# A chunked linear-attention layer and a product feed-forward on one core: a new written-out order, w loaded by SyncE, y in separate steps

## The chip, the cores and the metric

The kernel runs on one core of a Trainium2 chip. The metric is the device time of one execution in microseconds (us). The engines are TensorE (PE, with its weight loads PEld), VectorE (DVE), ScalarE (ACT), GpSimd (POOL) and SyncE (SP). SP and POOL issue the transfers.

## The reference

Inputs r, k, v, w have shape (batch 4, heads 8, steps 768, 48), in float32. For each batch and head a state of 48 x 48 runs over the steps:

```python
cur = np.einsum('bhd,bhe->bhde', u[None] * kt, vt)
y[:, :, t] = np.einsum('bhd,bhde->bhe', rt, state + cur)
state = wt[:, :, :, None] * state + np.einsum('bhd,bhe->bhde', kt, vt)
...
x = np.ascontiguousarray(attn_out.transpose(0, 2, 1, 3)).reshape(B * S, H * D)
...
a = x @ w1
b = x @ w2
h = a * b @ w3
return (h @ w_out).astype(np.float32)
```

x has 3072 rows of 384; w1 and w2 are 384 x 1024, w3 is 1024 x 1024, w_out 1024 x 384.

## The kernel before

The 768 steps are cut into 6 chunks of 128. A *unit* is one chunk of one or two batches: UNITS lists 13 of them. Units 0 and 1 have one batch (384 columns of heads times 48), the others two (768 columns). A step of the program is named after what it does and the number of its unit, `KRk_7` for one, and `ORDER`, a long string written out by hand or by a planner, gives each step with its engine, in the order in which it is issued. Each engine takes its own steps in that order and waits where data or a buffer isn't there yet. `BANKS` gives the PSUM bank of each step that needs one.

**Loads.** `win`, `kin`, `rin`, `vin` (L323) load a unit's slices. r, k and v are cast to bf16 on the way, w stays float32. w1 and w2 come in two column halves (L334, L338), w_out in one piece (L342), w3 in four pieces (L350). In the kernel before, SP issues `win_0` and `win_1` and POOL everything else that is loaded.

**The weights.** Since h is linear in a*b, w3 and w_out are multiplied once into one matrix w34: `wt` (L360) transposes w3 by matmuls, `w3Te` (L364) takes the result out of PSUM, `wm` (L369) multiplies by w_out, `w34e` (L374) takes that out. `warm` (L304) is a matmul on zeros.

**A unit.** ACT takes Ln of w (`ln`, L403). `cs` sums the logarithms over the chunk by a matmul with a triangle of ones (L415, columns for the whole chunk's decay L420). ACT then takes Exp: `pc` (the chunk's decay, L427), `ne` (the inverse, L434), and for units 3 to 12 `iw` (L478) and `e` (L486). Units 0 to 2 (`RAW`) get theirs transposed from the matmul `csT` (L452) and `et` (L458). DVE multiplies: `KRk` (L439), `rw` (L482), `KRr` (L490, L474), `rk` (L524), `ruk` (L544), and `dg` sums ruk over 48 (L550); `dv` multiplies v by it (L559, POOL or DVE). The scaled k and r are transposed, by PE (`trr`, `trk`: L469, L501, L516, with copies `trre`, `trke`: L505, L520) or by DMA transposes on SP (`dtr`, `dtk`: L495, L510).

`m` (L573) multiplies scaled k by scaled r in tiles of half height (64 x 128), one step per batch. The upper triangle of it is kept in bf16: by `msk` on DVE straight from PSUM (L592), or by `mcp`, a copy on ACT (L579), and then `maff`, on POOL (L587) or DVE (L585). `POOL_MASK` names those of the second kind.

`y` multiplies the chunk's r by the state (L608, half-height tiles) and the masked m by v (L614, full tiles) into the same PSUM banks, in one step. For units 0 to 2 (`Y_PE`) `yd` adds dv by a matmul (L624); for the others `yb` adds it as it takes y out of PSUM (L633; L630 without the addition). y is transposed by PE (`yt`, L652, with the copy `xT`, L656) or by DMA transposes on SP (`dty`, L642). `kv` (L668, tiles of half width) multiplies scaled k by v; `T`, `S` and `Sb` (L676, L681 to L685, L690) bring the state on.

**The feed-forward.** For each unit the steps `a` and `b` (L713) give blocks of x @ w1 and x @ w2, `asb` copies a's block out on ACT (L720), `abT` multiplies it by b's (L724, DVE), `o` multiplies by w34 (L730), `osb` takes that out of PSUM (L737), `st` stores it (L742, SP).

**ACT's table.** The first ACT step of the kernel before is `table`:

```python
nc.scalar.preload_act_table_set("natural_log_exp_and_others")
```

**Buffers.** r and k have 5 buffers each, v 6, w 4, masked m 4, xT 3, abT 3, a's block 3, outputs 4; most of what a unit holds else has 2. Which one a step takes goes round with the number of the unit or the block.

Of the kernel before, what the change touches and what calls it, by code (L numbers as in the profile page):

```python
# [35 lines left out]
BANKS = """
wt0=3 wm0=5 wt1=5 wm1=3 wt2=4 wm2=4 wt3=2 wm3=5 wt4=5 wm4=5 wt5=2 wm5=2 wt6=6 wm6=5 wt7=7 wm7=2 cs0=0 ct0=2 tr0=3
tk0=3 m0_0=0,1 y0=6,7 yt0=4 kv0=2 a0_0=0 b0_0=0 a0_1=0 b0_1=0 o0_0=5 cs1=1 ct1=0 tr1=6 tk1=1 m1_0=6,7 y1=0,1 yt1=4
kv1=3 a1_0=1 b1_0=1 a1_1=1 b1_1=1 o1_0=2 cs2=2,3 ct2=2,3 tr2=5 tk2=3 m2_0=3,4 m2_1=3,4 y2=3,4 yt2=4 kv2=0 a2_0=5
b2_0=6 a2_1=4 b2_1=2 a2_2=2 b2_2=5 a2_3=4 b2_3=3 o2_0=4 o2_1=3 cs3=3,4 tr3=0 tk3=1 m3_0=6,7 m3_1=0,1 y3=6,7 yt3=1  # L40
kv3=0 a3_0=1 b3_0=7 a3_1=2 b3_1=0 a3_2=0 b3_2=1 a3_3=2 b3_3=4 o3_0=0 o3_1=0 cs4=0,1 tr4=0 tk4=2 m4_0=5,6 m4_1=5,6
y4=6,7 yt4=1 kv4=3 a4_0=1 b4_0=5 a4_1=4 b4_1=1 a4_2=2 b4_2=4 a4_3=3 b4_3=5 o4_0=5 o4_1=2 cs5=0,1 tr5=1 tk5=5 m5_0=6,7
m5_1=0,1 y5=0,1 yt5=0 kv5=2 a5_0=5 b5_0=3 a5_1=4 b5_1=7 a5_2=4 b5_2=1 a5_3=0 b5_3=2 o5_0=3 o5_1=1 cs6=6,7 tr6=2 tk6=0
m6_0=6,7 m6_1=6,7 y6=6,7 yt6=6 kv6=4 a6_0=1 b6_0=0 a6_1=1 b6_1=5 a6_2=3 b6_2=4 a6_3=1 b6_3=2 o6_0=2 o6_1=0 cs7=2,3
m7_0=6,7 m7_1=6,7 y7=4,5 kv7=3 a7_0=2 b7_0=0 a7_1=1 b7_1=1 a7_2=0 b7_2=6 a7_3=3 b7_3=2 o7_0=2 o7_1=0 cs8=6,7 m8_0=6,7
m8_1=6,7 y8=6,7 kv8=1 a8_0=7 b8_0=3 a8_1=7 b8_1=6 a8_2=0 b8_2=6 a8_3=1 b8_3=0 o8_0=7 o8_1=0 cs9=4,5 m9_0=4,5 m9_1=0,1
y9=4,5 kv9=0 a9_0=2 b9_0=1 a9_1=2 b9_1=7 a9_2=3 b9_2=7 a9_3=6 b9_3=3 o9_0=7 o9_1=0 cs10=4,5 m10_0=6,7 m10_1=4,5
y10=4,5 kv10=2 a10_0=1 b10_0=3 a10_1=0 b10_1=6 a10_2=7 b10_2=7 a10_3=2 b10_3=1 o10_0=1 o10_1=1 cs11=2,3 m11_0=4,5
m11_1=2,3 y11=4,5 a11_0=0 b11_0=1 a11_1=0 b11_1=1 a11_2=3 b11_2=2 a11_3=1 b11_3=4 o11_0=3 o11_1=2 cs12=4,5 m12_0=4,5
m12_1=4,5 y12=6,7 a12_0=0 b12_0=3 a12_1=1 b12_1=3 a12_2=2 b12_2=0 a12_3=0 b12_3=3 o12_0=3 o12_1=2  # L50
# [4 lines left out]
kin_0@POOL ln_0@ACT warm6@2 cs_0@PE wo@POOL csT_0@PE pc_0@ACT et_0@ACT I128@POOL ne_0@ACT vin_1@POOL ublk@DVE warm6@1  # L55
wt_3_0@PE wt_0_0@PE vin_0@POOL wt_2_0@PE wt_1_0@PE win_2@POOL warm7@5 wt_2_1@PE wt_1_1@PE wt_0_1@PE w3Te_1@ACT
wt_3_1@PE KRk_1@DVE rin_2@POOL w3Te_0@DVE warm7@1 trk_1@PE trr_1@PE trke_1@ACT rk_1@DVE KRr_1@DVE u@POOL trr_0@PE
KRr_0@DVE m_1_0@PE mask@POOL KRk_0@DVE warm5@2 trk_0@PE rk_0@DVE kin_2@POOL msk_1_0@DVE trke_0@ACT warm5@2 m_0_0@PE
w3_2@POOL msk_0_0@DVE w1_0@POOL warm5@5 wm_1@PE w2_0@POOL wm_0@PE w1_1@POOL w3Te_3@ACT w34e_1@DVE y_0@PE w3Te_2@ACT
w34e_0@DVE y_1@PE win_3@POOL kv_0@PE kv_1@PE S_0@DVE wm_3@PE ln_2@ACT S_1@DVE Sb_1@DVE Sb_0@ACT w2_1@POOL csT_2@PE  # L60
w34e_3@ACT ruk_0@DVE vin_2@POOL wm_2@PE ruk_1@DVE et_2@ACT dg_0@DVE dg_1@DVE dv_0@DVE rin_3@POOL cs_2@PE w34e_2@DVE
trr_2@PE pc_2@ACT rk_2@DVE yd_0@PE ne_2@ACT dv_1@POOL KRr_2@DVE yb_0@ACT yt_0@PE yd_1@PE KRk_2@DVE w3_3@POOL wt_6_0@PE
wt_4_0@PE wt_7_0@PE xT_0@DVE wt_5_0@PE yb_1@DVE trk_2@PE ruk_2@DVE yt_1@PE kin_3@POOL a_0_0@PE trke_2@DVE xT_1@ACT
a_1_0@PE dg_2@DVE asb_0_0@ACT m_2_0@PE asb_1_0@ACT win_4@POOL msk_2_0@DVE b_0_0@PE b_1_0@PE abT_0_0@DVE m_2_1@PE
abT_1_0@DVE vin_3@POOL a_0_1@PE msk_2_1@DVE a_1_1@PE asb_0_1@ACT vin_6@POOL ln_3@ACT asb_1_1@ACT cs_3@PE ublk2@POOL
iw_3@ACT kin_5@POOL b_0_1@PE e_3@ACT b_1_1@PE pc_3@ACT ne_3@ACT abT_0_1@DVE kin_4@POOL abT_1_1@DVE kv_2@PE y_2@PE
S_2@DVE Sb_2@DVE rin_4@POOL rw_3@DVE KRr_3@DVE warm1@7 trr_3@PE trre_3@ACT win_5@POOL wt_4_1@PE wt_5_1@PE w3Te_4@ACT
wt_6_1@PE wt_7_1@PE w3Te_5@ACT vin_5@POOL wm_4@PE rk_3@DVE KRk_3@DVE ruk_3@DVE wm_5@PE rin_5@POOL ln_4@ACT w34e_4@DVE
w3Te_6@DVE iw_4@ACT dg_3@DVE cs_4@PE win_8@POOL w3Te_7@ACT wm_6@PE w34e_5@DVE e_4@ACT wm_7@PE vin_4@POOL pc_4@ACT
ne_4@ACT w34e_6@ACT dv_2@POOL kv_3@PE w34e_7@ACT trk_3@PE T_3@DVE o_1_0@PE trke_3@ACT S_3@POOL KRk_4@DVE win_6@POOL  # L70
yd_2@PE o_0_0@PE osb_1_0@DVE yb_2@DVE st_1_0@SP kin_6@POOL m_3_0@PE rk_4@DVE yt_2@PE osb_0_0@DVE rin_7@POOL m_3_1@PE
xT_2@ACT trk_4@PE ruk_4@DVE st_0_0@SP msk_3_1@DVE ln_5@ACT b_2_3@PE win_7@POOL trke_4@ACT a_2_1@PE rw_4@DVE rin_6@POOL
cs_5@PE msk_3_0@DVE iw_5@ACT a_2_2@PE asb_2_1@ACT dv_3@POOL a_2_0@PE e_5@ACT y_3@PE asb_2_2@ACT KRr_4@DVE kin_9@POOL
pc_5@ACT a_2_3@PE ne_5@ACT yb_3@DVE b_2_1@PE asb_2_0@ACT vin_8@POOL KRk_5@DVE trr_4@PE rw_5@DVE yt_3@PE trre_4@ACT
b_2_2@PE Sb_3@DVE xT_3@DVE vin_7@POOL b_2_0@PE KRr_5@DVE abT_2_2@DVE b_3_0@PE kin_7@POOL ln_6@ACT abT_2_0@DVE a_3_2@PE
abT_2_1@DVE asb_2_3@ACT m_4_1@PE a_3_0@PE dg_4@DVE iw_6@ACT win_10@POOL a_3_1@PE asb_3_0@ACT msk_4_1@DVE b_3_3@PE
dv_4@POOL asb_3_1@ACT b_3_2@PE abT_3_0@DVE m_4_0@PE abT_2_3@DVE win_9@POOL a_3_3@PE msk_4_0@DVE ln_7@ACT o_2_1@PE
kin_8@POOL asb_3_2@ACT rk_5@DVE asb_3_3@ACT abT_3_2@DVE y_4@PE iw_7@ACT kin_10@POOL abT_3_3@DVE b_3_1@PE osb_2_1@ACT
rw_7@DVE trr_5@PE st_2_1@SP rin_10@POOL ruk_5@DVE kv_5@PE trre_5@ACT yb_4@DVE kv_4@PE o_2_0@PE rin_8@POOL dg_5@DVE
T_4@DVE yt_4@PE dv_5@POOL osb_2_0@ACT trk_5@PE abT_3_1@DVE st_2_0@SP cs_6@PE xT_4@DVE trke_5@ACT o_3_0@PE rk_6@DVE  # L80
pc_6@ACT ne_6@ACT S_4@POOL T_5@DVE a_4_0@PE e_6@ACT ruk_6@DVE rin_9@POOL a_4_2@PE KRk_6@DVE Sb_4@ACT asb_4_0@ACT
dg_6@DVE a_4_3@PE kin_11@POOL osb_3_0@ACT b_4_1@PE ln_8@ACT rk_7@DVE st_3_0@SP rw_6@DVE win_11@POOL trk_6@PE
asb_4_2@ACT ruk_7@DVE a_4_1@PE iw_8@ACT KRr_6@DVE rin_11@POOL m_5_0@PE trke_6@ACT dv_6@DVE trr_6@PE b_4_0@PE
msk_5_0@DVE asb_4_1@ACT win_12@POOL o_3_1@PE trre_6@ACT abT_4_1@DVE m_6_0@PE abT_4_0@DVE osb_3_1@ACT b_4_2@PE
rin_12@POOL msk_6_0@DVE st_3_1@SP asb_4_3@ACT b_4_3@PE S_5@POOL m_5_1@PE abT_4_2@DVE cs_7@PE mcp_5_1@ACT vin_9@POOL
abT_4_3@DVE m_6_1@PE kv_6@PE dg_7@DVE e_7@ACT o_4_0@PE vin_10@POOL ne_7@ACT maff_5_1@DVE KRr_7@DVE pc_7@ACT
mcp_6_1@ACT y_5@PE KRk_7@DVE o_4_1@PE T_6@DVE osb_4_0@ACT dtr_7@SP vin_11@POOL Sb_5@ACT yb_5@DVE ln_9@ACT kv_7@PE
rk_9@DVE dtk_7@SP osb_4_1@ACT kin_12@POOL yt_5@PE rw_8@DVE iw_9@ACT cs_9@PE xT_5@DVE cs_8@PE st_4_1@SP e_9@ACT
rk_8@DVE b_5_3@PE st_4_0@SP maff_6_1@POOL ne_8@ACT a_5_3@PE pc_9@ACT pc_8@ACT e_8@ACT rw_9@DVE b_5_2@PE dv_7@POOL
T_7@DVE ne_9@ACT y_6@PE ln_10@ACT b_5_0@PE KRr_8@DVE ln_11@ACT a_5_1@PE S_7@POOL yb_6@DVE dtr_8@SP iw_10@ACT a_5_0@PE  # L90
vin_12@POOL ruk_8@DVE asb_5_1@ACT yt_6@PE ruk_9@DVE b_5_1@PE asb_5_0@ACT dg_8@DVE S_6@POOL xT_6@ACT a_5_2@PE
abT_5_0@DVE iw_11@ACT b_6_1@PE dv_8@DVE asb_5_2@ACT a_6_2@PE Sb_6@ACT abT_5_2@DVE b_6_2@PE asb_5_3@ACT abT_5_1@DVE
a_6_1@PE abT_5_3@DVE m_7_1@PE asb_6_1@ACT b_6_0@PE KRk_8@DVE asb_6_2@ACT abT_6_1@DVE dtk_8@SP o_5_1@PE mcp_7_1@ACT
# [702 lines left out]
```

## Time and profile before

| what | us |
|---|---|
| median of three runs | 178.04 |
| lowest and highest of them | 177.25, 178.37 |
| span of the profiled execution | 176.7 |
| PE busy | 159.3 |
| DVE busy | 131.3 |
| ACT busy | 97.9 |
| POOL busy, with its DMA issues | 92.8 |

The profiled execution shows its span, from the first to the last instruction; a time of its own beside the span isn't given for it. The share of an engine's busy time is an average over the whole span, and a busy PE isn't PE at its peak, since the ends of matmuls are modelled. The profile gives, besides, the span in 40 slices, the chain of work that ended last, groups of instructions by line with the mean length of one, and the DMA issues with their sizes.

### The profile page before, as it was taken

The numbers are of one execution on the slowest core, as the hardware profiler recorded it, in microseconds if no ns is written. First come the engines' busy times: TensorE is split into PE (matmuls) and PEld (weight loads), VectorE is DVE, ScalarE is ACT, GpSimd is POOL, SyncE is SP. The second block draws the span as 40 slices with busy tenths as digits, with TensorE's granted clock in tenths as the row PEclk, the third lists the DMA queues.
The fourth block names the chain that finished last, engine by engine and source line by source line (L and its number), as shares of the span: only waits on it lengthen the run. The fifth ranks groups of instructions, "written<-read, shape, count | busy, mean of one in ns | idle before, by whom it ended". The sixth has DMA issues, their size and how long they took to land.

```text
span 176.7 us, 4637 instructions
## 1 busy us (share of the span) xinstructions
PE 159.3 (90%) x1935; PEld 118.0 (67%) x1935; DVE 131.3 (74%) x209; ACT 97.9 (55%) x160; POOL 92.8 (53%) x91
## 2 busy tenths in 40 slices
...
DMA  5999999999999999999999997352745660151033
GB/s 95 171 164 192 190 195 211 221 177 192 139 169 186 226 192 147 190 170 177 223 193 143 190 120 142 100 125 67 147 108 121 132 153 1 26 156 45 4 113 111
DMA packets 104101, 25.70 MB, mean 145 GB/s; under 512 B 95216, under 2 KB 103024, under 8 KB 104080
## 3 DMA queue, kind: packets, MB, share of 16 engines
...
## 4 chain that ended last, share of the span: by engine, by line
PE 67%; DVE 15%; DMA 6%; ACT 5%; issue 3%; SPq 0%; DVEq 0%
PE banks L713 30%; PE banks L730 13%; PE banks L369 6%; DMA win<-in_w_dram 5%; PE banks L573 4%; DVE rk L524 2%; DVE abT L724 2%; PE banks L614 2%; PE banks L415 2%; PE banks L360 2%; DVE rw L482 2%; PE banks L304 2%; DVE Mbf L592 2%; DMA xT<-yb 1%; DVE ruk L544 1%
## 5 line engine op out<-in xcount | busy, mean ns | idle before, releaser
L713 PE MATMUL banks<-xT,w_bf 128*128 128x256 bf16 (+1 forms) x624 | 69.0, 264 | 1.7 <-DVE abT L724 0.8
L713 PEld LDWEIGHTS <-w_bf 128*128 128x128 bf16 x624 | 55.6, 98 | 10.2 <-issue 2.0
L720 ACT COPY a_sb<-banks 128x512 f32<-128x512 f32 x48 | 28.0, 594 | 28.4 <-PE banks L713 20.0
L724 DVE TENSOR_TENSOR abT<-a_sb,banks 128x512 bf16<-128x512 f32 x48 | 31.4, 679 | 11.3 <-PE banks L713 9.1
L730 PE MATMUL banks<-w,abT 128*128 128x384 bf16 x192 | 34.3, 326 | 0.0
L730 PEld LDWEIGHTS <-abT 128*128 128x128 bf16 x192 | 18.2, 98 | 10.7
L592 DVE TENSOR_TENSOR Mbf<-banks,mask 128x1024 bf16<-128x1024 f32 x16 | 19.5, 1216 | 3.7 <-PE banks L573 3.7
L559 POOL TENSOR_TENSOR dv<-vin,dg 128x768 bf16<-128x768 bf16 (+1 forms) x10 | 14.9, 1497 | 8.6 <-issue 5.5
L323 POOL DMA_DIRECT2D vin<-in_v_dram x13 | 14.6, 1123 | 5.6 <-issue 3.9
L323 POOL DMA_DIRECT2D win<-in_w_dram x11 | 12.9, 1176 | 6.6 <-issue 4.1
L323 POOL DMA_DIRECT2D kin<-in_k_dram x13 | 14.6, 1126 | 1.7 <-DMA w_bf<-in_moe_w_dram 1.0
L737 ACT COPY osb<-banks 128x384 f32<-128x384 f32 x16 | 7.8, 486 | 13.8 <-PE banks L730 13.8
L323 POOL DMA_DIRECT2D rin<-in_r_dram x13 | 14.5, 1119 | 0.6 <-DMA vin<-in_v_dram 0.3
L304 PE MATMUL banks<-zeros 128*128 128x512 bf16 x29 | 9.8, 461 | 3.4 <-DVE zeros L235 3.4
L403 ACT ACTIVATE lw<-win 128x768 bf16<-128x768 f32 (+1 forms) x13 | 10.4, 811 | 4.5 <-DMA win<-in_w_dram 4.5
L369 PE MATMUL banks<-wo_bf,w3T 128*128 128x384 bf16 x64 | 11.2, 326 | 1.1 <-ACT w3T L364 1.1
L587 POOL TENSOR_SCALAR_AFFINE_SELECT Mbf<-Mbf 128x1024 bf16<-128x1024 bf16 x4 | 4.8, 1188 | 14.3 <-ACT Mbf L579 14.3
L550 DVE TENSOR_REDUCE dg<-ruk 128x16 f32<-128x768 bf16 (+1 forms) x13 | 11.4, 879 | 0.0
L573 PE MATMUL banks<-KRT 64*128 64x128 bf16 x192 | 9.6, 218 | 1.0 <-ACT Mbf L579 0.5
L415 PE MATMUL banks<-lw,LT 128*128 128x384 bf16 x24 | 6.4, 341 | 4.3 <-ACT lw L403 4.3
L364 ACT COPY w3T<-banks 128x1024 bf16<-128x1024 bf16 x6 | 6.0, 1016 | 7.3 <-PE banks L360 3.7
L633 DVE TENSOR_TENSOR yb<-banks,dv 128x768 bf16<-128x768 f32 x10 | 9.5, 952 | 0.7 <-PE banks L614 0.4
...
## 6 DMA issues: line engine op xcount, KB each, us to landing
...
win<-in_w_dram POOLq DMA_DIRECT2D x11, 384.0 KB, 10.0
...
w_bf<-in_moe_w_dram POOLq DMA_DIRECT2D x4, 384.0 KB, 12.9
...
```

Of the source, the lines that this page charges most:

```text
L304: nc.tensor.matmul(banks[:, at, :], lhsT=zeros[:, :C], rhs=zeros, start=True, stop=True)
L323: QUEUE[eng].dma_start(dst, src)
L369: nc.tensor.matmul(one(f"wm{fi}")[:, :DM], lhsT=w3T[fi % 2][:, gi, :], rhs=wo_bf[:, gi, :], start=(gi == 0), stop=(gi == FI - 1))
L403: nc.scalar.activation(LW[:, :, :D], ww, Act.Ln)
L550: nc.vector.reduce_sum(dgs, ruks, axis=AX.X)
L559: e.tensor_mul(dvs, vv, dgs[:, :, None].to_broadcast([C, bh, D]))
L573: nc.tensor.matmul(o[:, e, q, :], lhsT=KRTs[a:a + PAD, 0, b * HP + q, :], rhs=KRTs[a:a + PAD, 1, b * HP + q, :], start=True, stop=True)
L592: nc.vector.tensor_mul(Mbf[m], mview(), mask.rearrange("s (j q) t -> s j q t", j=2))
L713: nc.tensor.matmul(o[:, f, :], lhsT=wt[:, di, fi * P:(fi + 1) * P], rhs=x[:, di, :T], start=(di == 0), stop=(di == DI - 1))
L720: copier(eng)(sa, one(f"a{t}_{g}"))
L724: nc.vector.tensor_mul(ab[:, g * per:(g + 1) * per, :T], sa.rearrange("p (f t) -> p f t", t=T), one(f"b{t}_{g}").rearrange("p (f t) -> p f ...
L730: nc.tensor.matmul(one(f"o{t}_{b}")[:, :DM], lhsT=ab[:, fi, b * C:(b + 1) * C], rhs=w34[:, fi, :], start=(fi == 0), stop=(fi == FI - 1))
```

## The change

The order is a new one, and so are the PSUM banks. With it:

- y falls into `ys` (state, one step per unit) and `yi` (masked m by v, one step per batch).
- w comes by SP for all units, `win_0` to `win_12`.
- w3's four pieces are now two blocks of 128 rows each, all columns; they were four blocks of rows and half of the columns.
- Transposes of r and k by DMA for units 5 to 12 (before 7 to 12), of y for units 2 and 4 to 12 (before 7 to 12).
- `Y_PE` and `N_PSUM` are empty: no `yd`, and `ne` writes bf16 to SBUF in all units.
- `POOL_MASK` has 14 masks (before 8); `S` may be on DVE.
- 5 abT buffers, 4 xT; which buffer of masked m, a's block and the output a step takes is now written out in `BANKS` (`M`, `sa`, `so`).
- 42 warm matmuls (before 29).
- u in columns and u in blocks, which nothing read, are gone, with code for options that no unit used.
- The step `table` stands late in the order, between `asb_9_1` and `asb_9_0`; the first ACT step is `ln_0`.

```diff
-N_X = 3
+N_X = 4
-N_AB = 3
+N_AB = 5
+N_W3 = 4
-N_PSUM = {0, 1, 2}
-DMA_R = {7, 8, 9, 10, 11, 12}
-DMA_K = {7, 8, 9, 10, 11, 12}
-DMA_Y = {7, 8, 9, 10, 11, 12}
+N_PSUM = set()
+DMA_R = {5, 6, 7, 8, 9, 10, 11, 12}
+DMA_K = {5, 6, 7, 8, 9, 10, 11, 12}
+DMA_Y = {2, 4, 5, 6, 7, 8, 9, 10, 11, 12}
-POOL_MASK = {(5, 1), (6, 1), (7, 1), (8, 1), (9, 1), (10, 1), (11, 1), (12, 1)}
-Y_PE = {0, 1, 2}
+POOL_MASK = {(1, 0), (2, 1), (4, 0), (4, 1), (5, 0), (6, 1), (7, 0), (7, 1), (8, 0), (9, 0), (9, 1), (10, 0), (11, 1), (12, 0)}
+Y_PE = set()
...
-win_1@SP table@ACT ones@DVE mask1@DVE win_0@SP w3_0@POOL ucol@SP w3_1@POOL padet@DVE padkr@DVE LT@POOL padlw@DVE
-kin_1@POOL zeros@DVE ln_1@ACT padr@DVE warm3@4 csT_1@PE rin_1@POOL cs_1@PE et_1@ACT rin_0@POOL pc_1@ACT ne_1@ACT
...
+zeros@DVE padr@DVE rin_0@POOL win_0@SP kin_1@POOL win_1@SP ones@DVE padlw@DVE ln_0@ACT LT@POOL ln_1@ACT mask1@DVE
+I128@POOL vin_0@POOL kin_0@POOL warm0@1 csT_0@PE rin_1@POOL warm1@2 trr_0@PE vin_1@POOL cs_0@PE win_2@SP cs_1@PE
+pc_0@ACT w3_1@POOL padet@DVE ln_2@ACT u@POOL pc_1@ACT csT_1@PE w3_0@POOL win_4@SP et_0@ACT ne_1@ACT warm5@7 trr_1@PE
...
+wm_7@PE rw_5@DVE ln_7@ACT KRr_5@DVE m_3_1@PE rw_6@DVE dv_2@DVE w1_0@POOL yb_2@DVE pc_6@ACT ne_6@ACT dty_2_0@SP
+msk_3_1@DVE e_6@ACT w34e_7@ACT rk_4@DVE m_4_0@PE ys_3@PE S_3@POOL w34e_6@ACT kv_4@PE maff_4_1@POOL a_1_1@PE
+mcp_4_0@ACT yi_3_0@PE cs_7@PE KRk_5@DVE a_0_1@PE yi_3_1@PE asb_1_1@ACT Sb_2@ACT rk_5@DVE Sb_3@ACT ruk_4@DVE a_1_0@PE
+w2_0@POOL w2_1@POOL KRr_6@DVE dty_2_1@SP T_4@DVE a_0_0@PE a_2_2@PE win_8@SP dtk_5@SP asb_0_1@ACT win_9@SP a_2_1@PE
+yb_3@DVE pc_7@ACT yt_3@PE maff_4_0@POOL dg_4@DVE ne_7@ACT asb_2_1@ACT b_2_1@PE b_1_0@PE e_7@ACT ys_4@PE abT_2_1@DVE
+xT_3@DVE kin_6@POOL b_1_1@PE dtr_5@SP asb_1_0@ACT dtr_6@SP win_10@SP abT_1_0@DVE ruk_5@DVE yi_4_0@PE ln_8@ACT
...
+maff_12_0@DVE a_9_3@PE o_6_1@PE asb_9_3@ACT yb_11@DVE asb_9_1@ACT table@ACT asb_9_0@ACT b_9_0@PE abT_9_3@DVE o_8_1@PE
...
-    for h in range(4):
-        f = slice(h // 2 * 4, h // 2 * 4 + 4)
-        gs = slice(h % 2 * 512, h % 2 * 512 + 512)
+    for h in range(N_W3):
+        f = slice(h * FI // N_W3, (h + 1) * FI // N_W3)
...
-            nc.gpsimd.dma_start(w3_bf[:, f, gs], w3r[:, f, gs])
+            nc.gpsimd.dma_start(w3_bf[:, f, :], w3r[:, f, :])
...
+        if c:
+            @op(f"ys_{t}")
+            def _(eng):
+                o = yv()
                 for b in range(nb):
                     for q in range(HP):
                         for e in range(2):
...
+        for b in range(nb):
+            @op(f"yi_{t}_{b}")
+            def _(eng, b=b):
+                o = yv()
+                M = Mbf[bank[f"M{t}_{b}"]]
                 for h in range(H):
...
-                elif c < NC - 2:
-                    nc.gpsimd.tensor_mul(Sp, Tp, PCb)
                 else:
-                    nc.gpsimd.tensor_mul(Bp, Tp, PCb)
+                    e = nc.gpsimd if eng == "POOL" else nc.vector
+                    e.tensor_mul(Sp if c < NC - 2 else Bp, Tp, PCb)
...
-                copier(eng)(sa, one(f"a{t}_{g}"))
+                copier(eng)(a_sb[bank[f"sa{t}_{g}"]], one(f"a{t}_{g}"))
...
-                copier(eng)(so, one(f"o{t}_{b}")[:, :DM])
+                copier(eng)(osb[bank[f"so{t}_{b}"]], one(f"o{t}_{b}")[:, :DM])
```

More of the change, by code (lines that the diff above doesn't have):

```diff
@@ L16 @@
 N_RIN = 5
+N_KIN = 5
 N_VIN = 6
@@ L42 @@
[L42 to L46, printed above, removed]
@@ L54 @@
-kin_1@POOL zeros@DVE ln_1@ACT padr@DVE warm3@4 csT_1@PE rin_1@POOL cs_1@PE et_1@ACT rin_0@POOL pc_1@ACT ne_1@ACT
[L55 to L93, printed above, removed]
@@ new lines @@
+I128@POOL vin_0@POOL kin_0@POOL warm0@1 csT_0@PE rin_1@POOL warm1@2 trr_0@PE vin_1@POOL cs_0@PE win_2@SP cs_1@PE
+pc_0@ACT w3_1@POOL padet@DVE ln_2@ACT u@POOL pc_1@ACT csT_1@PE w3_0@POOL win_4@SP et_0@ACT ne_1@ACT warm5@7 trr_1@PE
+et_1@ACT padkr@DVE KRk_1@DVE warm5@14 wt_2_0@PE ne_0@ACT cs_2@PE rk_1@DVE kin_2@POOL warm7@12 wt_1_0@PE KRr_0@DVE
+KRk_0@DVE wt_0_0@PE win_3@SP rk_0@DVE wt_1_1@PE KRr_1@DVE wt_0_1@PE kv_1@PE pc_2@ACT ne_2@ACT S_1@DVE trk_0@PE
+win_5@SP ruk_0@DVE trke_0@DVE csT_2@PE kv_0@PE rin_2@POOL wt_3_0@PE w3Te_1@ACT trk_1@PE wt_3_1@PE mask@POOL w3Te_0@DVE
@@ new lines @@
+ln_4@ACT S_0@DVE dg_0@DVE rk_2@DVE wo@POOL ruk_1@DVE rin_3@POOL KRk_2@DVE trr_2@PE trke_1@DVE warm1@6 trk_2@PE
+ln_3@ACT win_7@SP et_2@ACT iw_4@ACT iw_3@ACT m_0_0@PE wt_2_1@PE ruk_2@DVE trke_2@DVE KRr_2@DVE cs_3@PE dv_0@POOL
+pc_3@ACT msk_0_0@DVE wm_0@PE ne_3@ACT wm_1@PE m_1_0@PE ln_5@ACT w3Te_2@ACT rw_3@DVE w34e_0@DVE e_3@ACT cs_4@PE
+mcp_1_0@ACT cs_5@PE dg_1@DVE pc_4@ACT w3Te_3@DVE kin_3@POOL m_2_0@PE w34e_1@ACT pc_5@ACT KRk_3@DVE KRr_3@DVE
+msk_2_0@DVE ne_4@ACT rin_4@POOL wm_2@PE e_4@ACT vin_2@POOL ne_5@ACT trk_3@PE m_2_1@PE win_6@SP w3_2@POOL dv_1@DVE
@@ new lines @@
+trke_3@DVE mcp_2_1@ACT rk_3@DVE yi_0_0@PE maff_1_0@DVE kin_4@POOL w3_3@POOL wm_3@PE ln_6@ACT vin_3@POOL rw_4@DVE
+maff_2_1@POOL w34e_2@ACT yb_0@DVE dg_2@DVE e_5@ACT kv_2@PE wt_5_0@PE KRr_4@DVE yi_1_0@PE rin_5@POOL wt_5_1@PE Sb_1@ACT
+trr_3@PE wt_4_0@PE yb_1@DVE trr_4@PE w3Te_5@ACT w34e_3@ACT ruk_3@DVE Sb_0@DVE wt_4_1@PE KRk_4@DVE yt_0@PE trre_3@DVE
+S_2@DVE dg_3@DVE yt_1@PE rin_6@POOL wm_5@PE iw_5@ACT trk_4@PE wt_7_0@PE wt_6_0@PE w1_1@POOL trre_4@ACT w3Te_4@ACT
+wt_7_1@PE vin_4@POOL w34e_5@ACT dv_3@POOL m_3_0@PE trke_4@DVE xT_0@ACT xT_1@DVE wm_4@PE msk_3_0@DVE wt_6_1@PE kv_3@PE
```

234 lines of the change are left out of this document (102 added, 132 removed).

## The prediction

> **What bounds the kernel now.** I read the page's busy shares and slices first, then the chain that ended last, then busy times by stretch, then ScalarE's (ACT's) instructions in order of time.
>
> ```profile
> PE 159.3 (90%) x1935; PEld 118.0 (67%) x1935; DVE 131.3 (74%) x209; ACT 97.9 (55%) x160; POOL 92.8 (53%) x91
> ...
> DMA  5999999999999999999999997352745660151033
> GB/s 95 171 164 192 190 195 211 221 177 192 139 169 186 226 192 147 190 170 177 223 193 143 190 120 142 100 125 67 147 108 121 132 153 1 26 156 45 4 113 111
> ...
> PE 67%; DVE 15%; DMA 6%; ACT 5%; issue 3%; SPq 0%; DVEq 0%
> ```
>
> PE carries two thirds of the chain, and the DMA engines are full for the first 24 slices (24 x 4.42 = 106 us). ACT is on the chain for 5% and idle for 45%. An average hides stages, so I cut the span at two ACT steps, whose ends the time line gives: e_5 (60.3) and e_12 (126.1).
>
> ```profile
> 0.00:60.30 60.30, 49.02 (x561) 34.08 (x562) 36.95 (x70) 31.38 (x50) 46.08 (x52) 1.00 1.82 180
> 60.30:126.10 65.80, 63.42 (x855) 48.84 (x855) 62.96 (x95) 48.86 (x83) 42.12 (x36) 1.00 1.63 158
> 126.10:176.70 50.60, 46.89 (x522) 35.08 (x519) 31.38 (x46) 17.68 (x31) 4.61 (x4) 0.99 0.35 88
> ```
>
> The columns are the length, then busy PE, weight loads, DVE, ACT, POOL, the clock, DMA, GB/s. Stage 1 is bound by arriving data and dependences (no compute engine but PE over 61%), stage 2 by DVE (62.96 of 65.80, 96%), stage 3 by PE.
>
> The next lines are ACT's first ones, in order of time (start, length, instruction, idle before it).
>
> ```profile
> 0.80 1.28 ACT L231 ACT_TABLE_LOAD   x1 [0.80 <-PEq L780]
> 3.60 0.52 ACT L403 ACTIVATE lw<-win 128x384 bf16<-128x384 f32 x1 [1.51 <-DMA win<-in_w_dram]
> 5.79 0.60 ACT L458 ACTIVATE ETt<-banks 128x512 bf16<-128x512 f32 x1 [1.66 <-PE banks L452]
> ```
>
> The one table load of the whole run is the step `table`. It names a set that serves Ln (L403) and Exp (L458) alike, stands ahead of both, and costs 1.28 us in time that ACT would have waited anyway.
>
> The last lines are pieces of the chain of waits (start, length, what).
>
> ```profile
> 85.29 0.33 PE banks L573 x8
> ...
> 107.51 0.66 PE banks L713 x6
> 108.16 0.33 PE banks L573 x8
> 108.49 0.76 PE banks L713 x6
> ...
> 145.28 0.55 PE banks L573 x16
> ```
>
> Six L713 matmuls take 0.66, or 0.76 behind the half-height L573 ones; two L573 steps in a row take 0.55 where two single ones take 2 x 0.33. So each change of tile shape costs 0.10 to 0.11 us.
>
> **The change, part by part.** Prices are row means, for PE the chain's pieces (a or b step of six matmuls 0.66, o and wm 1.30, m 0.33, cs 0.51, eight transposes 0.45, warm 0.24).
>
> *Shape changes.* Counting shapes along the PE steps gives 78 changes before, 50 after: 28 x 0.10 = 2.8 us less PE.
>
> *Transposes.* yt_2, 4, 5, 6 (4 x 0.33), trr and trk of units 5 and 6 (4 x 0.45) and the three yd (0.66) leave PE: 3.8 us. For them SP issues 12 more DMA transposes, 1.25 us each, 15 us of an engine that has little else. They land in 3.2 us (median), but the slowest took 8.5 us, beside running loads. The new ones run there too: I take 8.5. dty_2_1 is two issues and one landing behind yb_2, 11 us; between yi_2_1 and a_2_2 PE has only 6 us of other steps, so some 5 us of wait may open there.
>
> *w by SyncE.* POOL loses 11 issues x 1.18 = 12.9 us, SP gains 11 x 0.5. The bytes are the same and DMA is full, so it brings nothing directly. It may shorten DVE: one rk took 2.67 us beside POOL's maff and dv, where its least was about half a microsecond. I count 0 and keep up to 3 us for the range. On SP a later win stands behind dty, dtk and st; all have four buffers of slack until ln needs them: 0, at worst one landing (10 us).
>
> *w3 in row pieces, new load order.* The pieces stay at 512 KB. But w2_1, by which b_2_1 and b_1_1 start, is now behind all of w3, wo, w1 and 26 unit loads. With the KB of the issue table that is 2048 + 768 + 1536 (weights) + 1152 (r) + 960 (k) + 768 (v) + 2688 (w) + 96 (u) = 10.0 MB. The GB/s row, summed slice by slice, reaches 9.4 MB at 53 us and 10.2 at 57. So PE can't be past its first 41 us of work before 57 us, a delay of 16; before, PE stood at the same work about as late (below). Gain 0.
>
> *The mask, y, state.* msk on DVE falls from 16 to 10 (-7.3 us); ACT gets 6 copies of 1.02, POOL 6 affine selects of 1.19. S moves four times from POOL to DVE (+2.2). yd gone makes yb an addition at the same price. Separate ys and yi move no work. Five abT and four xT buffers add no instruction. 13 more warm matmuls (3.1 us) lie in the head, where PE waits for w3. All of it is in the sums below.
>
> *The table step.* `table` moves behind the last Exp. What set is active when ln_0 runs is then not asked for by the program. I take that each need is met by itself: a set for Ln at ln_0, another for Exp at pc_0, and so on, because a step that names the joint set would not be needed if that set came unasked. Along the new ACT order the Ln and Exp steps alternate in 22 groups, 12 of them by e_7, 10 from there to e_12; with `table` itself 23 loads against 1, at 1.28 us each 28 us more for ACT. Bounds for one load: from below 0, where it falls into a wait of ACT; from above 1.28 plus 0.86, if the ACTIVATE before (row of L403) must be out first. I take 1.28, the row itself.
>
> **The sum.** I cut the new order where PE has the same work behind it: e_7 (43.8 us of PE steps, against 43.4 at e_5 before), then e_12. Steps counted by kind times row means, before against after, ACT without table loads:
>
> - stage 1: PE 43.4, 43.8; DVE 37.8, 42.9; ACT 33.0, 40.2
> - stage 2: PE 61.6, 51.6; DVE 68.6, 58.7; ACT 56.3, 41.5
> - stage 3: PE 45.7, 54.5; DVE 35.0, 38.5; ACT 18.3, 22.2
>
> Row means overlap; measured busy is 0.91 of such a sum on ACT in stage 1 and 0.87 in stage 2.
>
> Stage 1: 40.2 x 0.91 + 12 x 1.28 = 52 us of ACT, where it had 31 in 60.3. Eight microseconds would be left for its waits, which were 29. The first 3 to 4 (first win) stay, as do those for wo and the late w3 pieces; I take 13 us of waits: 65. Without loads it would be 57 (w2) plus the dty_2 wait, about 60.
>
> Stage 2: DVE's 58.7 at the pace of before (65.8 for 68.6) is 56.3. ACT is at 41.5 x 0.87 + 12.8 = 49, nearly as full as DVE, and each feeds the other through PE: 2 more, 58.3.
>
> Stage 3: PE 54.5, plus before's 50.6 - 45.7 = 4.9 of stalls and tail, less 1 for shape changes: 58.4.
>
> Sum 65 + 58.3 + 58.4 = 181.7. The profiled execution has a span of 176.7; the median of the three runs, 178.04, is 1.3 above it, and I take that as what lies around the span: 183.0.
>
> **The rivals.**
>
> 1. *No loads but one* (the other side). If the set found for ln_0 serves Exp too, nothing is added: 60 + 56.3 + 58.4 + 1.3 = 176.0, and 172 if the dty_2 wait closes and DVE is less disturbed by POOL. For it: one load served all activations before. Against: that set was asked for by name. It decides at the second Exp step. Its price is the whole 7 us between 183 and 176. By the Trainium skill (ScalarE: Activation LUTs, Table sets: the hidden batching unit) an Ln followed by an Exp needs a single load, since one shipped set has both; by that rule this rival holds. The trace agrees only for a program that names that set. Chance 0.17.
>
> 2. *Loads hidden.* ACT waits 29 us in stage 1; if nearly all the loads fall there, stage 1 is 61 and stage 2 56.5: 177 to 178. Against: the loads stand between ln and its Exps, on the way of every unit. Chance 0.13.
>
> 3. *Loads dearer.* At the upper bound, 2.14, ACT has 62 us in stage 1 (72 with 10 of waits), 57 in stage 2 (62): 72 + 62 + 58.4 + 1.3 = 194. The Trainium skill (the same page, What ACT_TABLE_LOAD costs) gives 2.66 us for a switch, drain included; by it the estimate would be about 205. No run here shows a switch. Chance 0.12.
>
> 4. *Data late.* dty_2, win or w2_1 some 5 us later than I have them, without loads: 181. Chance 0.08.
>
> **How the numbers follow.** My forecast, 183 (own range 179 to 191), has the other 0.50. A measurement of this kernel tells about 1% from no change, 176.3 to 179.8. Faster: 0.10 of rival 1 and 0.03 of rival 2. Same: 0.07 of rival 1, 0.10 of rival 2. Slower: 0.50 + 0.12 + 0.08 = 0.70. The range: 174 leaves out the better half of rival 1 (0.08), 199 the worse part of rival 3 (0.08).
>
> **What would show it.** Right: 23 rows of ACT_TABLE_LOAD at 1.28 us; ACT busy near 120 us; e_7 ending at 62 to 68; DVE over 90% between e_7 and e_12; half-height steps in pairs of 0.55. Wrong: one load and ACT under 100 us (rival 1); 23 loads and e_7 by 61 (rival 2); idle time on ACT behind every load (rival 3); PE waiting for xT or w_bf from DMA with ACT idle (rival 4). If stage 3 is short although stage 1 was long, my cut at equal PE work was wrong.

## The result, and the profile after

The changed kernel takes 211.16 us (median of four runs, 209.97 to 211.91); the kernel before took 177.87 us beside it. The ratio is 1.188 [1.183, 1.193]: 33 us slower, where 183 us and at most 199 had been forecast. The profiled execution has a span of 210.2 us. Ratios, here and below, leave out the few executions that ran slower at a lower granted clock; medians hold them.

The page of the changed kernel, the lines that answer to those shown of before, and its DMA queues (packets, MB, share of 16 engines' time):

```profile
PE 165.8 (79%) x1884; PEld 121.4 (58%) x1886; DVE 125.7 (60%) x210; ACT 122.7 (58%) x178; POOL 81.2 (39%) x78
...
PEclk9987966969799999985998899999999999999998
DMA  8999999999996999999999999999995502401234
...
q0 software_dynamic: 78224, 11.64, 79.0%
q1 hardware_dynamic: 53456, 15.60, 47.5%
...
PE 15%; DVE 2%; issue 0%; ACT 0%; ACTq 0%
```

No engine is near its limit: PE fell from 90% to 79%, DVE from 74% to 60%, and only ACT rose, by 24.8 us, some less than its 22 added loads of 1.28. The DMA row is at 9 in nearly all of the first 30 slices of 5.26 us, to 158 us instead of 106. The second queue, which had 23600 packets before, has 53456. PE's clock, at 9 before in every slice but the last, drops to 0.5 to 0.8 in ten slices; it is lowest in the slice in which PE's longest wait, 6.52 us, ends. Time went into waiting, not into work; the chain that ended last covers only the last sixth of the span, so the waits have to be read stage by stage.

The stretches cut as forecast, at the ends of e_7 and e_12 (length, then busy PE, weight loads, DVE, ACT, POOL, clock, DMA, GB/s):

```profile
0.00:76.70 76.70, 55.39 (x598) 36.32 (x601) 39.96 (x77) 51.11 (x71) 41.03 (x46) 0.89 1.51 147
76.70:149.10 72.40, 55.22 (x712) 42.95 (x710) 48.69 (x80) 49.75 (x71) 33.23 (x29) 0.93 1.74 145
149.10:210.20 61.10, 55.20 (x580) 42.17 (x577) 37.03 (x55) 21.82 (x38) 6.93 (x5) 0.99 0.41 94
```

Forecast were 65, 58.3 and 58.4. The first two stages lost 12 and 14 us, the third 3. In the second stage DVE, which was to be over 90% busy, is at 67%.

ACT in order of time, around unit 8's logarithm (start, length, instruction):

```profile
61.27 1.28 ACT L383 ACT_TABLE_LOAD   x1
62.56 0.84 ACT L383 ACTIVATE lw<-win 128x768 bf16<-128x768 f32 x1
63.42 1.28 ACT L407 ACT_TABLE_LOAD   x1
```

Each of these loads starts 0.02 us after the instruction before it ended, and the ACTIVATE 0.01 us after its load: a switch costs 1.3 us here, and no time for emptying ACT is seen. There are 11 such loads ahead of Ln, 11 ahead of Exp, and the one of `table`: 23, as counted.

The issue table (KB each, median us from issue to landing) and, of the tile KRT, the landing of its DMA transposes:

```profile
win<-in_w_dram SPq DMA_DIRECT2D x11, 384.0 KB, 9.6
kin<-in_k_dram POOLq DMA_DIRECT2D x11, 192.0 KB, 14.6
rin<-in_r_dram POOLq DMA_DIRECT2D x11, 192.0 KB, 16.8
vin<-in_v_dram POOLq DMA_DIRECT2D x11, 192.0 KB, 14.4
```

```profile
DMA to landing us min/median/max: 3.1/8.1/12.3
```

Before, k, r and v landed in 9.7, 9.4 and 10.8 us, and KRT in 3.0/3.2/8.5. So v became slower by a third, k by half, r by more, and the transposes took over twice as long, with nearly the same bytes (27.5 MB against 25.7); w, now on SP's queue, did not (10.0 before).

How one such landing becomes idle PE is seen in three views. First POOL's issue of `kin_7`, the piece of k for unit 7, and the landing of this one issue:

```profile
77.36 1.17 POOL L310 DMA_DIRECT2D kin<-in_k_dram  x1
...
DMA to landing us min/median/max: 17.3/17.3/17.3
```

DVE, in the time line:

```profile
94.73 0.56 DVE L419 TENSOR_TENSOR KR<-kin,NEt 128x768 bf16<-128x768 bf16 x1 [7.52 <-issue]
95.21 0.68 DVE L679 TENSOR_TENSOR abT<-a_sb,banks 128x512 bf16<-128x512 f32 x1
```

PE:

```profile
95.94 4.00 PE L669 MATMUL banks<-xT,w_bf 128*128 128x256 bf16 x18 [6.52 <-DVE abT L679]
```

KRk_7 on DVE (L419) multiplies that piece. It waits for two transfers: the piece, which landed at 94.7, and the transpose of unit 5's scaled k, whose buffer it writes and which had landed by 78.0. The time line names no releaser ("issue"), but the late piece of k fits to 0.1 us. DVE stood 7.5 us behind it, the a*b product queued behind KRk_7 came late, and PE waited 6.5 us for it.

SP's queue was behind at the same time:

```profile
82.27 4.95 SPq L310 DMA_DIRECT2D win<-in_w_dram  x2
87.31 7.20 SPq L485 DMA_TRANSPOSE KRT<-KR  x1
```

The input of that transpose (unit 6's scaled k) was ready at 82.6, but two pieces of w stood ahead of it on SP, and the transpose then kept SP for 7.2 us.

### The profile page after: what moved, and what is told of

It is laid out like the page before. It is cut to its first block, busy times and chain, and to the rows that moved or that the text cites. A ratio compares the mean times of both kernels' runs of the same rounds, so it can differ in the third digit from the quotient of the medians.

```text
span 210.2 us, 4569 instructions
## 1 busy us (share of the span) xinstructions
PE 165.8 (79%) x1884; PEld 121.4 (58%) x1886; DVE 125.7 (60%) x210; ACT 122.7 (58%) x178; POOL 81.2 (39%) x78
## 5 line engine op out<-in xcount | busy, mean ns | idle before, releaser
L669 PE MATMUL banks<-xT,w_bf 128*128 128x256 bf16 (+1 forms) x624 | 72.5, 270 | 15.4 <-DVE abT L679 11.8
L544 POOL TENSOR_SCALAR_AFFINE_SELECT Mbf<-Mbf 128x1024 bf16<-128x1024 bf16 x10 | 13.1, 1307 | 37.8 <-ACT Mbf L536 37.8
L518 POOL TENSOR_TENSOR dv<-vin,dg 128x768 bf16<-128x768 bf16 (+1 forms) x8 | 12.2, 1527 | 39.8 <-DVE dg L509 32.2
L536 ACT CAST Mbf<-banks 128x1024 bf16<-128x1024 f32 x14 | 14.3, 1023 | 8.4 <-PE banks L530 8.4
L419 DVE TENSOR_TENSOR KR<-kin,NEt 128x768 bf16<-128x768 bf16 (+1 forms) x13 | 7.4, 572 | 18.8 <-ACT NEt L414 9.5
L293 PE MATMUL banks<-zeros 128*128 128x512 bf16 x40 | 14.5, 516 | 1.5 <-DVE zeros L239 1.3
L549 DVE TENSOR_TENSOR Mbf<-banks,mask 128x1024 bf16<-128x1024 f32 x10 | 12.2, 1217 | 3.0 <-PE banks L530 2.9
L593 DVE TENSOR_TENSOR yb<-banks,dv 128x768 bf16<-128x768 f32 (+1 forms) x13 | 11.6, 890 | 3.4 <-issue 3.2
L457 DVE TENSOR_TENSOR rw<-rin,iw 128x768 bf16<-128x768 bf16 x10 | 7.5, 754 | 9.4 <-DMA rin<-in_r_dram 8.5
L530 PEld LDWEIGHTS <-KRT 64*128 64x128 bf16 x192 | 6.5, 100 | 9.6 <-issue 9.0
```

What stands on the lines that cost most here:

```text
L293: nc.tensor.matmul(banks[:, at, :], lhsT=zeros[:, :C], rhs=zeros, start=True, stop=True)
L518: e.tensor_mul(dvs, vv, dgs[:, :, None].to_broadcast([C, bh, D]))
L530: nc.tensor.matmul(o[:, e, q, :], lhsT=KRTs[a:a + PAD, 0, b * HP + q, :], rhs=KRTs[a:a + PAD, 1, b * HP + q, :], start=True, stop=True)
L536: copier(eng)(Mbf[bank[f"M{t}_{b}"]], mview())
L544: nc.gpsimd.affine_select(x, x, compare_op=Alu.is_gt, fill=0.0, base=0, channel_multiplier=-1, pattern=[[0, 2 * HP], [1, C]])
L669: nc.tensor.matmul(o[:, f, :], lhsT=wt[:, di, fi * P:(fi + 1) * P], rhs=x[:, di, :T], start=(di == 0), stop=(di == DI - 1))
```

## The experiments

Every time is a median with its ratio to the kernel before, measured on the same chip (there 177.2 to 177.7 us). Token lines of the order are shown by what moved; line numbers of a kernel with a step more or less differ by one from the changed kernel's.

### One burden undone in the changed kernel, or added to the kernel before

Two pairs test the loads of the tables and w's queue from both sides.

```diff
 changed kernel, table first
+table@ACT zeros@DVE padr@DVE rin_0@POOL
...
-asb_9_1@ACT table@ACT asb_9_0@ACT
+asb_9_1@ACT asb_9_0@ACT
```

> The changed kernel with one step moved back: table is ACT's first step, as before the change; all else stays. One table load in place of 23, so 28 us less of ACT. Theory L (the loads are most of the loss): 180 to 185 us. Theory T (transfers are most of it: w by SyncE and the added DMA transposes make the loads of r, k, v land after 15 us instead of 9): 200 to 205 us. If both matter about alike: about 192.

206.73 us, ratio 1.166 [1.160, 1.172]. One load instead of 23 gives back 4.4 us: the loads are a small part of the loss, and the time lies above even the range of Theory T. The DMA row is still at 9 up to the 30th slice, and PE's longest wait is now 6.9 us for a DMA transpose of KR.

```diff
 kernel before, table behind the last Exp
-win_1@SP table@ACT ones@DVE
+win_1@SP ones@DVE
...
+e_12@ACT table@ACT
```

> The kernel before, with table moved behind the last Exp (e_12) and nothing else changed: 25 loads in place of one. Theory L: 195 to 205 us. Theory T: the loads fall mostly into ACT's waits (45% of the span), 181 to 185 us.

200.34 us, 1.130 [1.124, 1.137]. In the order of before, the same kind of loads (25) costs 23 us, as Theory L had it and five times as much as in the changed kernel. A price of one load in us is thus no property of the load: it depends on what else the order waits for.

```diff
 changed kernel, table first, and
-win_2@SP ... win_12@SP
+win_2@POOL ... win_12@POOL
```

> The changed kernel with table first and, besides, win_2 to win_12 issued by POOL at the same places in the order (win_0 and win_1 stay on SP). Theory L: the same as the run with table first alone, within 1%. Theory T: 10 to 20 us faster than that run, since r, k, v and the DMA transposes no longer share the engines with w's small packets: 182 to 190 us.

201.30 us, 1.134 [1.129, 1.140]: 5.4 us less than with w by SyncE, between the two expectations.

```diff
 kernel before
-win_2@POOL ... win_12@POOL
+win_2@SP ... win_12@SP
```

> The kernel before with win_2 to win_12 issued by SP at the same places in the order, nothing else changed. Theory L: 176 to 179 us, no difference. Theory T: loads of r and k land later than the 9 us of before, 183 to 195 us. A third possibility: a win stands behind st on SP's queue and comes late, which would show as ACT waiting for win.

191.67 us, 1.080 [1.077, 1.084]: 14 us for the same bytes from another queue, as Theory T had it. Its DMA queues:

```profile
q0 software_dynamic: 79248, 11.64, 87.1%
q1 hardware_dynamic: 46304, 13.77, 43.6%
```

Before, q0 had 80480 packets and q1 23600. The 4.3 MB of w took only 1232 packets off POOL's queue, but put 22704 on SP's: 11 pieces of 128 x 16 rows are 22528, so there each row of 48 numbers (192 bytes) is a packet of its own. The pieces of r, k and v landed in 17.1, 15.5 and 16.7 us, those of w in 13.1.

```diff
 kernel before
-DMA_R = {7, 8, 9, 10, 11, 12}
-DMA_K = {7, 8, 9, 10, 11, 12}
-DMA_Y = {7, 8, 9, 10, 11, 12}
+DMA_R = {5, 6, 7, 8, 9, 10, 11, 12}
+DMA_K = {5, 6, 7, 8, 9, 10, 11, 12}
+DMA_Y = {2, 4, 5, 6, 7, 8, 9, 10, 11, 12}
```

> The kernel before, with the twelve added DMA transposes alone: r and k of units 5 and 6, y of units 2, 4, 5 and 6 go by SP in place of PE, at the same places in the order. Theory X (DMA transposes beside running loads are dear: they wait for the loads and slow them): 182 to 192 us, KRT landing in a median of 5 us or more. Theory O (the loss that is left, 24 us with one table load and w by POOL, lies in the new order itself): 177 to 181 us.

213.85 us, 1.203 [1.196, 1.210]: the twelve transposes alone cost 36.7 us there, above both expectations. They stood at the places of PE's transposes, without a lead. In the median the transfers were little slower here, against Theory X: KRT landed in 3.4 us and xT in 3.3 instead of 2.4 (10.6 and 8.4 at most), r, k and v in 11.1, 9.3 and 11.3. What cost was that PE waited for landings, 24.2 us in seven waits for xT alone. Two of PE's waits, in the time line:

```profile
65.11 2.72 PE L713 MATMUL banks<-xT,w_bf 128*128 128x256 bf16 x12 [8.79 <-DMA xT<-yb]
...
107.79 0.61 PE L573 MATMUL banks<-KRT 64*128 64x128 bf16 x8 [6.68 <-DMA KRT<-KR]
```

Twelve a-matmuls that took 1.48 us before take 2.72 behind the wait, and the granted clock in that stretch of 10 us was 0.52: this wait cost PE a second time. (Behind its wait of 2.85 us for xT the changed kernel's twelve took 1.47.)

```diff
 changed kernel, table first, w by POOL, and
-DMA_R = {5, 6, 7, ...}   (DMA_K, DMA_Y alike)
+DMA_R = {7, ...}
-dtk_5@SP ... dtr_5@SP dtr_6@SP ... dty_4_0@SP dty_4_1@SP
+trk_5@PE trke_5@ACT ... trr_5@PE trre_5@ACT ... yt_4@PE xT_4@DVE
```

> The changed kernel with one table load, w by POOL, and the twelve transposes back on PE, in free PSUM banks at or just behind their places. Theory X: 183 to 190 us, most of the 24 us that are left gone. Theory O: 197 to 202 us, as without this step.

190.96 us, 1.080 [1.075, 1.085]: another 10.3 us, a little above what Theory X expected. All three burdens are gone, but 14 us are still there. From here on this is "the undone kernel".

```diff
 kernel before, the three edits above together
+e_12@ACT table@ACT
+win_2@SP ... win_12@SP
+DMA_R = {5, 6, ...}
```

> The kernel before with all three put in: 25 table loads, win_2 to win_12 by SP, the twelve DMA transposes. If the three costs add (23 and 14 us measured one by one, and the third) it comes to 215 us or more; if they overlap, to 203 to 212. What it differs from the changed kernel's 211 is what the new order, the mask split, the weights' order and the buffers bring.

228.39 us, 1.291 [1.283, 1.299]. The three cost 51 us together, against 23 + 14 + 37 = 74 one by one, so they overlap in part (the expectation's bounds were drawn before the third was known to cost 37). The changed kernel carries the same burdens, with two loads fewer, in 17 us less: its order, or what else came with it, does stand up to them better.

### What the new order loses by itself

By 40 us PE had done 22.1 us of work before and 15.2 in the undone kernel (busy time without the warm-up products), since the first w3 rows come behind six pieces of r, k and v.

```diff
 undone kernel
-zeros@DVE padr@DVE rin_0@POOL
+zeros@DVE padr@DVE w3_1@POOL w3_0@POOL rin_0@POOL
...
-warm5@14
+warm5@4
-warm7@12
+warm7@4
-padet@DVE ln_2@ACT u@POOL
+padet@DVE u@POOL
-ne_0@ACT cs_2@PE
+ne_0@ACT ln_2@ACT cs_2@PE
```

> The changed kernel with its three burdens undone (table first, w by POOL, the twelve transposes on PE) still took 14 us more than the kernel before. By its trace PE had done 6.9 us less real work than in the kernel before after 40 us (busy time without the warm-up products: 15.2 against 22.1), because the first rows of w3 were asked for behind six pieces of r, k, v and stood ready at 19.7 instead of 12.4 us. Here those two loads come first on POOL, the third tile's logarithm comes behind the first tile's exponentials on ACT, and 18 warm-up products go. Theory Start (the late w3 is what the new order loses in its first 40 us, and what is lost there is not caught up): 183 to 186 us, the first transposes of w3 before 14 us. Theory Order (the start is slack for the later stages, and the loss sits in the order between 60 and 120 us): 189 to 191 us, with the real work at 40 us above 20 and the loss appearing later.

188.28 us, 1.060 [1.055, 1.065]: 2.7 us less, between the two expectations. The wait only changed its name:

```profile
11.10 0.61 PE L445 MATMUL banks<-I,rin 128*128 128x128 bf16 x4 [4.52 <-DMA rin<-in_r_dram]
...
25.56 1.04 PE L445 MATMUL banks<-I,rin 128*128 128x128 bf16 x8 [3.60 <-DMA rin<-in_r_dram]
```

Now r comes late behind w3: both are wanted in the same microseconds.

```diff
 changed kernel, only the twelve transposes on PE again
+DMA_R = {7, ...}
+trk_5@PE trke_5@ACT ...
```

> The changed kernel with only its twelve added DMA transposes put back on PE; the table loads, and w by SyncE, stay. Theory Transposes (beside the second queue's w they are the largest burden, since each waits for a full DMA): 192 to 199 us. Theory Overlap (the burdens hide one another, so that taking away one leaves the wait to the next): 203 to 208 us, with PE still waiting for r and k or for ACT.

209.60 us, 1.176 [1.168, 1.185], above both expectations. It can't be told from the changed kernel. The transfers did recover: r, k and v landed in 7.4, 7.5 and 6.4 us, faster than in the kernel before, and KRT in 3.2. With loads and w left in place other waits took over: PE's largest are now 7.5 us for r and 3.5 for w3.

```diff
 kernel before
-N_X = 3
+N_X = 4
-N_AB = 3
+N_AB = 5
```

> The kernel before with five buffers for a*b instead of three and four for x instead of three, and nothing else. Theory Slack (the buffers are part of the intended gain): 174 to 176 us. Theory None (no row of the kernel before shows a wait for a buffer of a*b, its waits of DVE there being on PE's results): 177 to 178 us.

177.51 us, 1.000 [0.996, 1.004]: the buffers alone do nothing, as no wait for one had been seen.

### The supply of data taken out

What the three burdens share is the DMA engines. A row of 48 numbers is 192 bytes, and r, k, v and w are laid out so that the next row of the same step lies elsewhere. These runs read each piece of r, k, v and w from one stretch of DRAM instead of in rows of 48 numbers; bytes, instructions and waits stay, the numbers that land are others of the same tensor.

```diff
-            src = ROW[x][b0:b0 + nb, :, c * C:(c + 1) * C, :].rearrange("b h t d -> t (b h) d")
+            n0 = (c * 4 + b0) * C * H * D
+            src = ROW[x].rearrange("b h t d -> (b h t d)")[n0:n0 + nb * C * H * D].rearrange("(t x d) -> t x d", t=C, d=D)
```

> The kernel before, but each piece of r, k, v and w is read from one stretch of DRAM of the same size, so that a partition's row is one long piece instead of 8 or 16 rows of 48 numbers; what lands are other numbers of the same tensor, so the result is of other data, while bytes, instructions and waits stay. It takes the supply of data out of the time. Theory Supply (the pieces' short rows bound the kernel's first 100 us): 163 to 170 us, since PE is busy for 159 us of the span and some of its first 20 us cannot start sooner. Theory Order: 174 to 177 us.

177.21 us, 0.998 [0.995, 1.002], the kernel before with this reading: no gain, against 163 to 170 if the supply bound it. Its page:

```profile
DMA  4999999999969995999999627353745660151033
...
q0 software_dynamic: 34304, 15.96, 65.7%
q1 hardware_dynamic: 21808, 9.44, 23.3%
```

POOL's queue has 34304 packets instead of 80480 and takes 65.7% instead of 107.5%, and yet the time is the same. The pieces of r, k and v landed in 6.5 to 7.7 us instead of 9.4 to 10.8, and nothing came of it. The kernel before was not bound by how fast these pieces come, although its DMA row showed 9 for 23 slices. That row shows 9 here too: it tells that transfers are under way, not that more could not be had.

> The same reading in long rows in the changed kernel with its three burdens undone (191 us). Theory Supply (the new order's remaining 14 us are data that come late to a stage that needs more of them first, w1 and w2 being asked for at 45 to 54 instead of 18 to 23 us): within 5 us of the kernel before that reads so. Theory Order (they are waits among the engines): 10 us or more above it still.

184.49 us, 1.039 [1.033, 1.045], the undone kernel, between its two expectations: 6.5 of its 14 us were data that came late, 7.3 were not.

> The same reading in long rows in the changed kernel, its table loads, its w by SyncE and its twelve DMA transposes all kept. Theory Supply (the DMAs being full is what makes the transposes and w dear, and what the loads of the tables fall together with): 180 to 188 us, the transposes landing in 3 to 4 us again, and the loads of the tables worth 10 to 20 us over the undone kernel that reads so. Theory Burdens (the transposes and the loads cost by themselves): 195 us or more.

195.24 us, 1.097 [1.088, 1.106], the changed kernel as it is: 16 of its 34 us go when the rows are long, but the burdens still cost 10.7 over the undone kernel, and the time lies at the lower bound of Theory Burdens. Its issue table and KRT:

```profile
win<-in_w_dram SPq DMA_DIRECT2D x11, 384.0 KB, 6.5
kin<-in_k_dram POOLq DMA_DIRECT2D x11, 192.0 KB, 7.4
rin<-in_r_dram POOLq DMA_DIRECT2D x11, 192.0 KB, 9.6
```

```profile
DMA to landing us min/median/max: 3.1/5.9/13.0
```

The transposes did not get back to the expected 3 to 4 us.

> The changed kernel with the third to the last piece of w asked for by POOL and nothing else undone. Theory Queue (w's short rows on a second queue are the largest burden that stands alone: the pieces of r, k and v land in 15 instead of 9 us): 200 to 204 us. Theory Overlap (each burden alone is hidden by the two others, as with the transposes, whose undoing gave under 2 us): 206 to 210 us.

The edit is w by POOL alone, with short rows again. 209.31 us, 1.173 [1.164, 1.181]: 2 us, so w alone is hidden by the others as well. Here too r, k and v came back to 8.4, 8.1 and 7.8 us in the median. So it took w by SyncE and the added transposes together to bring these landings to 14 to 17 us in this order, and a median can hide the piece that counts: `kin_7` took 25.0 us to land in this run, and KRk_7 waited 9.5 us for it.

With long rows the last burdens were told apart.

> The changed kernel that reads r, k, v and w in long rows (195 us), with the table loaded first, so that the 22 other loads go; the twelve DMA transposes and w by SyncE stay. With long rows the burdens still cost 10.7 us together over the undone kernel (184.5). Theory Loads (with the data there in time, the loads stand on the way from logarithm to exponential and are most of what is left): 185 to 189 us. Theory Transposes (their landing, 6 us for r and k even here, is most of it): 192 to 195 us.

185.69 us, 1.044 [1.040, 1.049]. Without the 22 loads the long-row kernel is 9.5 us faster, as Theory Loads had it, and can't be told from the undone one (1.039 [1.033, 1.045]), though the twelve transposes and w by SyncE are still in it.

> The same long-row kernel with only the twelve transposes put back on PE; the 23 loads and w by SyncE stay. Theory Loads: 192 to 196 us. Theory Transposes: 185 to 189 us.

196.8 us in the two executions that the ratio is of (198.53 in the median of four), 1.108 [1.101, 1.114]: taking the transposes off SP gains nothing there.

> The undone kernel with w3 asked for first and 18 fewer warm-up products (188.3 us with short rows), reading in long rows. Of its first form (184.5 with long rows) 7 us over the kernel before were left with the supply taken out. Theory Start (the order's first 20 us, where r waits behind w3 or w3 behind r, hold them): 178 to 181 us. Theory Chain (they sit between 60 and 120 us, where DVE waits for ACT's copies of a): 183 to 185 us.

182.84 us, 1.028 [1.024, 1.033], with w3 first: the start holds some 1.7 us, 5.6 are left over the kernel before. From 60 to 80 us PE's busy time (second number) is 16.41 in this kernel

```profile
60.00:80.00 20.00, 16.41 (x229) 13.81 (x229) 14.85 (x23) 13.52 (x22) 10.44 (x13) 1.00 1.14 149
```

and the whole 20 us in the kernel before that reads so:

```profile
60.00:80.00 20.00, 20.00 (x262) 16.01 (x260) 20.00 (x34) 14.56 (x24) 12.03 (x14) 1.00 1.25 159
```

PE stands idle for 3.6 us there and for none in the kernel before, the largest difference in a stretch of 20 us. It is a place to look and not a share of the 5.6: the two kernels don't stand at the same work there. The transposes put back on PE stand there, and their copies on ACT; whether those or the order make this wait was not tried.

> The kernel before with w from SyncE (191.7 us with short rows), reading r, k, v and w in long rows, so that the 22528 packets of 192 bytes that the second queue got become 1408 long ones. Theory Short rows (what w by SyncE costs is the time of its short packets beside those of r, k and v): 177 to 179 us, as the kernel before reads in long rows. Theory Queue (the cost is in SyncE's issues or in the second queue itself): 187 us or more.

179.54 us, 1.011 [1.005, 1.017], the kernel before with w by SyncE and long rows; its queues:

```profile
q0 software_dynamic: 33424, 11.64, 58.5%
q1 hardware_dynamic: 23392, 13.77, 29.6%
```

The pieces of r and k landed in 8.2 and 7.0 us. Of the 14 us that w by SyncE cost, 12 are gone, and the time lies half a microsecond above Theory Short rows. For those 12 it was neither SyncE nor its queue, it was the short packets. This run made the rows of all four tensors long, so it doesn't tell w's packets from those of r, k and v beside them.

## Why the prediction was wrong, step by step

The experiments cut the 34 us between 177.2 and 211.2 as follows. Each number is what is left when the burdens go in this order; in another order the shares differ, because the burdens overlap.

| taken out | time | share |
|---|---|---|
| nothing (the changed kernel) | 211.2 | |
| short rows | 195.2 | 16.0 |
| and 22 table loads | 185.7 | 9.5 |
| and the twelve DMA transposes, w by SyncE | 184.5 | 1.2, not told from 0 |
| and the late w3 | 182.8 | 1.7 |
| the kernel before, long rows | 177.2 | 5.6 open |

*w by SyncE, and DMA taken as a fixed bound: the step that failed.* "The bytes are the same and DMA is full, so it brings nothing directly" counted 0; measured were 14 us in the kernel before and 5.4 in the changed kernel with one table load. The step failed twice. The bytes are the same but the packets are not: 22704 more on the second queue, 12 of the 14 us in the kernel before. And the row of nines was no bound: the long-row run shows room under it in the kernel before, and in the changed kernel 16 us go when the rows are long. What I took as a bound already paid for was slack, and the change used it up. The Trainium skill (DMA: Bandwidth & Descriptors, SWDGE vs HWDGE vs iDMA) gives plain transfers to SP or ACT and leaves GpSimd the irregular ones; for w's rows of 192 bytes the measurement decides against it, by 14 us in the kernel before. The same page of the Trainium skill (Specifications) wants 512 bytes in a transfer for full rate; the runs agree with it, since with rows of 3072 bytes for w the loss is 2 us.

*Transposes.* "I take 8.5" for a landing was near (KRT's median became 8.1), but I charged it to one step, dty_2, at 5 us, and there PE waited only 2.85. What the sum lacked is elsewhere: the landing of the old transposes and of r, k and v rose as well, and the wait for the late piece of k (KRk_7, 7.5 us) was not among my waits. "1.25 us each" of "an engine that has little else" failed too: a transpose of k held SP for 3.66 us in the median, one piece of w for 4.3 us, and what stood behind them on SP was asked for late. Undone last, the twelve are worth 10.3 us (201.3 to 191.0); undone alone, not told from 0; alone in the kernel before, 37 us.

*The loads.* 23 at 1.28 us and an ACT of 122.7 us (near 120 forecast) were right, and so was the fall of rivals 1 and 3. The 7 us of the forecast stand between the two measured shares, 4.4 with short rows and 9.5 with long ones. The rule of the Trainium skill that rival 1 weighed (ScalarE: Activation LUTs, Table sets: the hidden batching unit), one load for an Ln followed by an Exp, doesn't hold for this program: each change between Ln and Exp loaded anew. Nor do the 2.66 us for a switch that the same page of the Trainium skill gives (What ACT_TABLE_LOAD costs): it was 1.3. A sum of durations could not show that the order of before would lose five times as much by them (23 us).

*The sum.* Taken out one by one with the data as they are, the terms compare so. The loads were put at 7 us and gave 4.4; w was put at 0 and gave 5.4 (206.7 to 201.3); the transposes were put at dty_2's wait and gave 10.3; and the order that is left was to gain some 5 us and lost 13.8. (The 5 is an estimate: 176.0 without loads, less some 3 of dty_2's wait in stage 1, is 173, against 178.0 before.) So the largest miss lies in the stage sums. Each stage got the row means of its engines and the waits of before, and nothing for data that come later than before. In stage 2 the price was DVE's, since I read 62.96 us of 65.80 as its bound; PE, at 63.42, was as full, and the row can't tell which of the two bounded the stage.

With long rows the changed kernel's stages end at e_7 by 71.1 us and at e_12 by 132.0, with 62.3 after it. Against 65, 58.3 and 58.4 the sum was 12 us short with the data there in time, and 28 with the data as they are. "Gain 0" for the new load order left out its loss: 6.5 of the 13.8 us of the undone kernel go with long rows. Rival 4, data late, had the right mechanism at a chance of 0.08, and at "some 5 us" it was a third of the 16 us measured.

*Shape changes.* Forecast 2.8 us less PE, and 0.7 for the three yd. The undone kernel, with the same transposes as before, has 160.2 us of busy PE with 13.5 of warm-up products, the kernel before 159.3 with 9.8: 2.8 us less, where 3.5 were forecast. The intended gain is there, and it lies in an engine that now waits. Where half-height steps run in pairs, they take 0.62 us in the time line's lengths, where two single ones take 2 x 0.40 (0.87 and 1.04 for the two pairs behind a wait).

*The sign* was right, but the reason given for it, the loads alone, is 4 to 10 of the 34 us. What should have shown the forecast wrong did: DVE at 67% in the second stage instead of over 90%, e_7 ending at 76.7 instead of 62 to 68, and PE waiting for xT from DMA (2.85 us), the mark of rival 4, and for r (up to 3.6 us), with the loads there as well. The two were held to exclude each other, and both came.

What stays open: the last 5.6 us, how the three burdens share the 16 us that go with long rows, and why undoing w or the transposes alone brings the median landings back but little of the time. No run gave a kernel faster than the kernel before.
